# Values of all 40 rows of a segment computed in the softmax wait, in two column groups, in a recurrent-memory transformer block

## The chip, the cores and the metric

One core of one Trainium2 chip. The metric is the device time of one execution of the whole program, in microseconds (us), as the median of several executions. PE is TensorE, DVE is VectorE, ACT is ScalarE, POOL is GpSimd, SP is SyncE, which only issues DMAs here.

## The reference, cut to what matters

A forward and backward pass of a block: layernorm, attention with a recurrent memory, layernorm, gated FFN. The part that this case touches is the forward attention. It walks 64 segments of 32 rows; each segment also sees 8 memory rows, and these are the attention output of the segment before. Segment s + 1 therefore can't start before segment s has ended.

```python
# S = 2048 rows, D = 448, H = 16 heads of 256 (4096 columns), M = 8, seg = 32, L = 40
for s in range(n_seg):                      # 64 dependent steps
    h = concat([mem, x[s*32:(s+1)*32]])     # 40 rows
    q, k, v = h @ Wq, h @ Wk, h @ Wv        # each 40 x 4096
    p = softmax(mask(q k^T * scale))        # per head, 40 x 40
    o = (p v) @ Wo                          # 40 x 448
    mem = o[:8]                             # goes to the next segment
    outs.append(o[8:])
# then h = x + outs, layernorm, FFN, and the gradients of everything
```

Of the kernel before, what the change touches and what calls it, by code (L numbers as in the profile page):

```python
# [15 lines left out]
P = 128  # L16
# [130 lines left out]
def run_all(k: _K):  # L147
    nc, tc, ctx = k.nc, k.tc, k.ctx
    S, D, M, H, Dh, HD, F = k.S, k.D, k.M, k.H, k.Dh, k.HD, k.F
    SEG, L, NSEG, NT, KC, DP, MC, DC, FC = k.SEG, k.L, k.NSEG, k.NT, k.KC, k.DP, k.MC, k.DC, k.FC  # L150
    assert MC == 32 and DC == 2 and H == 16 and M == 8 and NSEG % 16 == 0 and D == 448 and F == 1792
    aps = k.aps
    k.Wq2 = aps["A_Wq"].rearrange("d h e -> d (h e)")
    k.Wk2 = aps["A_Wk"].rearrange("d h e -> d (h e)")
    k.Wv2 = aps["A_Wv"].rearrange("d h e -> d (h e)")
    k.Wo2 = aps["A_Wo"].rearrange("h e d -> (h e) d")

    const = ctx.enter_context(tc.tile_pool(name="const", bufs=1))
    dram = ctx.enter_context(tc.tile_pool(name="dram", bufs=1, space=bass.MemoryType.DRAM))
    k._small = ctx.enter_context(tc.tile_pool(name="small", bufs=4))  # L160
    k.f32p = ctx.enter_context(tc.tile_pool(name="f32", bufs=1))
    arena = ctx.enter_context(tc.tile_pool(name="arena", bufs=1))
    psum = ctx.enter_context(tc.tile_pool(name="psum", bufs=1, space=bass.MemoryType.PSUM))
    k.W = _Arena(arena, "arW", 124)
    k.A = _Arena(arena, "arA", 65)
    k.B = _Arena(arena, "arB", 9.25)
    k.ps1 = lambda: psum.tile([P, 512], FP32, tag="ps", name="psf", bufs=5)
    k.fx1 = lambda: psum.tile([P, 512], FP32, tag="fx", name="fx", bufs=2)
    k.po1 = lambda: psum.tile([P, 512], FP32, tag="po", name="po", bufs=1)
    k.ph1 = lambda: psum.tile([P, 1024], BF16, tag="po", name="ph", bufs=1)  # L170

    def f32(tag, n, name):
        return k.f32p.tile([P, n], FP32, tag=tag, name=name)
    k.f32 = f32

    ident = const.tile([P, P], BF16)
    make_identity(nc, ident[:])
    identf = const.tile([P, P], FP32)
    make_identity(nc, identf[:])
    k.ident = ident  # L180
    k.identf = identf
    sel = const.tile([P, 32], FP32)
    nc.vector.tensor_tensor(out=sel[:], in0=identf[:, 0:32], in1=identf[:, 32:64], op=ALU.add)
    nc.vector.tensor_tensor(out=sel[:], in0=sel[:], in1=identf[:, 64:96], op=ALU.add)
    nc.vector.tensor_tensor(out=sel[:], in0=sel[:], in1=identf[:, 96:128], op=ALU.add)
    k.sel = sel
    maskb = const.tile([P, L], FP32)
    nc.gpsimd.memset(maskb[:], 0.0)
    mask1 = const.tile([L, L], FP32)
    nc.gpsimd.memset(mask1[:], 0.0)  # L190
    nc.gpsimd.affine_select(out=mask1[:], in_=mask1[:], compare_op=ALU.is_ge, fill=-1e9,
                            base=0, pattern=[[-1, L]], channel_multiplier=1)
    nc.gpsimd.memset(mask1[:, SEG:L], 0.0)
    nc.gpsimd.memset(mask1[SEG:L, :], 0.0)
    nc.sync.dma_start(out=maskb[0:L, :], in_=mask1[:])
    nc.sync.dma_start(out=maskb[64:64 + L, :], in_=mask1[:])
    k.maskb = maskb
    eps_t = const.tile([P, 1], FP32)
    nc.gpsimd.memset(eps_t[:], 1e-5)
    k.eps_t = eps_t  # L200
    k.rstd1 = const.tile([P, NT], FP32, name="rstd1")
    k.rstd2 = const.tile([P, NT], FP32, name="rstd2")
    k.mv2 = const.tile([P, NT, nc.vector.BN_AGGR_DIM], FP32, name="mv2")

    def dt(name, shape, dtype=BF16):
        return dram.tile(shape, dtype, name=name)
    W2 = MC * 64
    NB = NT + NSEG // 16
    k.NB = NB
    dr = dict(XN=dt("XN", [NB * P, DP]), Hh=dt("Hh", [S, D]), HN=dt("HN", [S, D]), DH=dt("DH", [S, D], FP32),  # L210
              DHb=dt("DHb", [NB * P, DP]), Zt=dt("Zt", [S, F]), DGP=dt("DGP", [S, F]), DU=dt("DU", [S, F]),
              Vx=dt("Vx", [S, HD]), QT=dt("QT", [NSEG, P, W2]), KT=dt("KT", [NSEG, P, W2]),
              VG=dt("VG", [NSEG, P, W2]), P_all=dt("P_all", [NSEG, P, 8 * L]), DXN=dt("DXN", [S, D], FP32),
              X_o=dt("X_o", [NB, P, MC * P]), HC=dt("HC", [NB * P, DP]))
    for nm in ("q", "k", "v"):
        dr["X_" + nm] = dt("X_" + nm, [NT, P, MC * P])
        dr["M_" + nm] = dt("M_" + nm, [NT, P, MC * 32])
    k.dr = dr

    forward_chain(k)  # L220
    ffn_phase(k)
    backward_chain(k)
    tail_phase(k)
# [39 lines left out]
def forward_chain(k: _K):  # L263
# [17 lines left out]
    stg_b = [A(24 + 4 * i, 2048) for i in range(2)]  # L281
    xblk_b = [A(32 + 8 * i, 32, P) for i in range(2)]
    mblk = A(48, 32, P)
    hT_roll = A(56, KC, NWIN, L)
    hx_b = [A(59.75 + i, KC, P) for i in range(2)]
    v_sb = A(61.75, 1024)
    mh = A(63.75, KC, P)
    memT_pad = B(0, KC, 32)
    PT_bd = B(0.25, 8, 2, L)
    o8_b = [B(1.5 + 0.5 * i, 32, M) for i in range(2)]  # L290
    x2_b = [B(2.5 + 0.875 * i, D) for i in range(2)]
# [4 lines left out]
    nc.vector.memset(qT_b[1][:, :, L:64], 0.0)  # L296
    nc.vector.memset(kT_b[0][:, :, L:64], 0.0)
    nc.vector.memset(kT_b[1][:, :, L:64], 0.0)
    nc.gpsimd.memset(memT_pad, 0.0)
    nc.gpsimd.memset(PT_bd, 0.0)  # L300
    for i in range(2):
        nc.gpsimd.memset(V_b[i], 0.0)
    om = k.f32("f1", DP, "om")
    nc.gpsimd.memset(om[:], 0.0)
    pO = k.po1()
    nc.vector.memset(pO[:], 0.0)

    m0 = h_b[0]
    nc.sync.dma_start(out=v_sb[0:M, 0:D], in_=MEM0)
    nc.vector.memset(v_sb[0:M, D:DP], 0.0)  # L310

    def stats(t):
        q = nc.sync if t % 2 == 0 else nc.scalar
# [16 lines left out]
    pm = k.ps1()  # L330
    pmh = pm[:].bitcast(BF16)
    for kc in range(KC):
        nc.tensor.transpose(pmh[:, kc * M:(kc + 1) * M], v_sb[0:M, kc * P:(kc + 1) * P], ident[0:M, 0:M])
    pm3 = pmh[:, 0:KC * M].rearrange("p (c m) -> p c m", m=M)
    nc.vector.tensor_copy(out=hT_roll[:, :, 0, SEG:L], in_=pm3)
    nc.scalar.copy(out=memT_pad[:, :, 0:M], in_=pm3)
    for t in range(2, NT):
        stats(t)

# [11 lines left out]
    def stg():  # L351
        rot[0] += 1
        return stg_b[rot[0] % 2]

    def v_proj(t, n0, n1):
        if t >= NT:
            return
        for nn in range(n0, n1, 4):
            sg = stg()
            for n in range(nn, nn + 4):  # L360
                pv = k.fx1()
                for kc in range(KC):
                    nc.tensor.matmul(pv[:, 0:512], lhsT=hx_b[t % 2][:, kc, :], rhs=Wv_sb[:, kc, n * 512:(n + 1) * 512],  # L363
                                     start=(kc == 0), stop=(kc == KC - 1))
                k.evac(sg[:, (n - nn) * 512:(n - nn + 1) * 512], pv[:, 0:512])
            nc.gpsimd.dma_start(out=dr["Vx"][t * P:(t + 1) * P, nn * 512:(nn + 4) * 512], in_=sg)

    def load_v(s):
        if s >= NSEG:
            return  # L370
        for g in range(2):
            nc.sync.dma_start(out=V_b[s % 2][64 * g:64 * g + SEG, :],
                              in_=dr["Vx"][s * SEG:(s + 1) * SEG, g * 2048:(g + 1) * 2048])

    def wpass(W_sb, s, dst):
        sl = s % NWIN
# [16 lines left out]
            nc.gpsimd.dma_start(out=dr["X_o"][t][:, hf * 2048:(hf + 1) * 2048], in_=ot)  # L393

    prep_tile(0)
    v_proj(0, 0, 8)
    prep_tile(1)
    v_proj(1, 0, 8)
    load_v(0)
    for s in range(NSEG):  # L400
        t, r = divmod(s, 4)
        jm = s % 16
# [5 lines left out]
        with k.prio.crit():  # L408
# [3 lines left out]
            for h in range(8):  # L412
                for g in range(2):
                    for dc in range(DC):
                        j = 2 * (2 * h + dc) + g
                        nc.tensor.matmul(pS[64 * g:64 * g + 64, h * L:(h + 1) * L], lhsT=qT[:, j, :], rhs=kT[:, j, 0:L],
                                         start=(dc == 0), stop=(dc == DC - 1), skip_group_check=True)
            pV = [k.ps1() for _ in range(2)]
            for b in range(2):
                for kc in range(KC):  # L420
                    for j in range(4):
                        n = 2 * j + b
                        nc.tensor.matmul(pV[b][32 * j:32 * j + 32, 0:512], lhsT=memT_pad[:, kc, :],  # L423
                                         rhs=Wv_sb[:, kc, n * 512:(n + 1) * 512],
                                         start=(kc == 0), stop=(kc == KC - 1), skip_group_check=True)
            S_sb = k.f32("f2", 8 * L, "S_sb")[:].rearrange("p (h n) -> p h n", n=L)
# [4 lines left out]
            nc.vector.tensor_reduce(out=mx[:], in_=S_sb, axis=AX.X, op=ALU.max)  # L431
            nc.vector.tensor_tensor(out=S_sb, in0=S_sb, in1=mx[:].unsqueeze(2).to_broadcast([P, 8, L]), op=ALU.subtract)
            nc.scalar.activation(out=S_sb, in_=S_sb, func=ACT.Exp)
            k.evac(v_sb[:, 0:512], pV[0][:, 0:512], "s")
            k.evac(v_sb[:, 512:1024], pV[1][:, 0:512], "s")
            for j in range(4):
                g = j // 2
                eng = nc.sync if j % 2 == 0 else nc.scalar
                eng.dma_start(out=Vs[64 * g + SEG:64 * g + L, (j % 2) * 1024:(j % 2 + 1) * 1024],
                              in_=v_sb[32 * j:32 * j + M, :])  # L440
            ssum = smal.tile([P, 8], FP32, name="ssum")
            nc.vector.tensor_reduce(out=ssum[:], in_=S_sb, axis=AX.X, op=ALU.add)
            rs = smal.tile([P, 8], FP32, name="rs")
# [26 lines left out]
            if s + 1 < NSEG:  # L470
# [5 lines left out]
                                     start=True, stop=True)  # L476
                pm3 = pm[:, 0:KC * M].rearrange("p (c m) -> p c m", m=M)
                nc.vector.tensor_copy(out=hT_roll[:, :, (s + 1) % NWIN, SEG:L], in_=pm3)
                nc.scalar.copy(out=memT_pad[:, :, 0:M], in_=pm3)

        load_v(s + 1)
        nc.gpsimd.dma_start(out=dr["QT"][s], in_=qT.rearrange("p c n -> p (c n)"))
        nc.sync.dma_start(out=dr["KT"][s], in_=kT.rearrange("p c n -> p (c n)"))
        nc.gpsimd.dma_start(out=dr["P_all"][s], in_=P_sb.rearrange("p h n -> p (h n)"))
# [2 lines left out]
        nc.gpsimd.tensor_copy(out=mblk[:, :, jm * M:(jm + 1) * M], in_=o8)  # L487
        if r == 0:
            prep_tile(t + 2)
        if r % 2 == 1:  # L490
            v_proj(t + 2, 4 * (r // 2), 4 * (r // 2) + 4)
        if r == 3:
            px = k.fx1()
            for j in range(MC):
# [577 lines left out]
```

## The kernel before: the parts that the change and the argument touch

Scheduling is automatic: each engine gets a fixed order of instructions, and `k.prio.crit()` gives what stands in it the first claim. Everything else, such as `v_proj` and the output projection of a finished row tile (`px`, not shown), is put into the gaps as filler. `k.ps1()` takes the next of 5 PSUM banks in turn. `k.evac(..., "s")` copies PSUM to SBUF on ACT, "v" on DVE.

The values of the 32 sequence rows don't depend on memory, so this kernel makes them 128 rows at a time, ahead of need, writes them to DRAM and loads each segment's share:

```python
    def v_proj(t, n0, n1):                  # one row tile of 128 rows, 512 columns at a time
        ...
                for kc in range(KC):
                    nc.tensor.matmul(pv[:, 0:512], lhsT=hx_b[t % 2][:, kc, :], rhs=Wv_sb[:, kc, n * 512:(n + 1) * 512], ...)
                k.evac(sg[:, (n - nn) * 512:(n - nn + 1) * 512], pv[:, 0:512])
            nc.gpsimd.dma_start(out=dr["Vx"][t * P:(t + 1) * P, nn * 512:(nn + 4) * 512], in_=sg)

    def load_v(s):
        for g in range(2):
            nc.sync.dma_start(out=V_b[s % 2][64 * g:64 * g + SEG, :], in_=dr["Vx"][s * SEG:(s + 1) * SEG, g * 2048:(g + 1) * 2048])
```

Only the 8 memory rows' values are made inside the segment. They are made in four column groups of the array, and so land on partitions 0, 32, 64 and 96; four small DMAs move them to partitions 32 and 96 of the value tile:

```python
            wpass(Wq_sb, s, qT); wpass(Wk_sb, s, kT)      # q^T and k^T: 256 small matmuls in all
            ...                                           # scores: 32 matmuls into pS
            pV = [k.ps1() for _ in range(2)]
            for b in range(2):
                for kc in range(KC):
                    for j in range(4):
                        n = 2 * j + b
                        nc.tensor.matmul(pV[b][32 * j:32 * j + 32, 0:512], lhsT=memT_pad[:, kc, :],
                                         rhs=Wv_sb[:, kc, n * 512:(n + 1) * 512], ...)
            ...                                           # scale+mask, max, subtract on DVE
            nc.scalar.activation(out=S_sb, in_=S_sb, func=ACT.Exp)
            k.evac(v_sb[:, 0:512], pV[0][:, 0:512], "s")
            k.evac(v_sb[:, 512:1024], pV[1][:, 0:512], "s")
            for j in range(4):
                g = j // 2
                eng = nc.sync if j % 2 == 0 else nc.scalar
                eng.dma_start(out=Vs[64 * g + SEG:64 * g + L, (j % 2) * 1024:(j % 2 + 1) * 1024],
                              in_=v_sb[32 * j:32 * j + M, :])
            ...                                           # sum, reciprocal, multiply: P_sb
            pPT = k.ps1()                                 # P^T by 16 matmuls with the identity
            for g in range(2):
                k.evac(PT_bd[64 * g:64 * g + L, :, g, :], pPT[64 * g:64 * g + L, ...], "vs"[g])
            ...                                           # heads: 16 matmuls, lhsT = Vs, rhs = PT_bd
            ...                                           # o8 <- memory rows of the heads; pO = o8 @ Wo (32 matmuls)
            ...                                           # om <- pO (DVE, then ACT); sum and transpose; new memory into hT_roll, memT_pad
```

## Time and profile before

| | before |
|---|---|
| time, median of 3 | 3683.66 us (3679.29 to 3687.23) |
| span of the profiled run | 3670.7 us |
| first FFN matmul | 1388 us |
| mean granted clock, 100 to 1388 us | 0.91 |

The top of the page: the span, the busy time of each engine, and the PE clock in 40 slices of the span, in tenths of full speed.

```profile
span 3670.7 us, 122624 instructions
PE 3122.9 (85%) x55484; PEld 2044.1 (56%) x55550; DVE 1349.2 (37%) x2969; ACT 955.4 (26%) x2197; POOL 547.1 (15%) x1177
...
PEclk9999999999999868998799999999999888999999
```

PE looks 85% busy, and its clock is near full almost everywhere, but that alone says nothing about the forward part: there a segment can't overlap the next one, and what counts is which wait ends last in each. The timeline of one segment shows it. Columns: start, duration, engine, line, operation, output and inputs, count, and in brackets the idle time before and what ended it. "SPq" and "PEld" are issuing and weight loading.

```profile
610.75 1.91 PE L423 MATMUL psf<-arW,arB 128*32 128x512 bf16 x31
610.87 0.49 DVE L427 SCALAR_TENSOR_TENSOR S_sb<-psf,maskb 128x320 f32<-128x320 f32 x1 [0.54 <-PE psf L416]
611.84 0.58 ACT L77 CAST arA<-psf 128x512 bf16<-128x512 f32 x1 [2.27 <-PE psf L423]
612.82 0.57 ACT L77 CAST arA<-psf 128x512 bf16<-128x512 f32 x1
613.41 1.51 SPq L439 DMA_DIRECT2D arA<-arA  x2
613.70 0.49 DVE L445 TENSOR_TENSOR arB<-S_sb,rs 128x320 bf16<-128x320 f32 x1
614.25 0.38 PE L449 MATMUL psf<-ident,arB 128*40 128x40 bf16 x16 [1.59 <-DVE arB L445]
615.18 0.42 ACT L77 CAST arB<-psf 40x320 bf16<-40x320 f32 x1 [1.80 <-DVE arB L75]
616.80 0.73 PE L457 MATMUL psf<-arB,arA 128*128 128x80 bf16 x16 [2.18 <-issue]
617.60 3.16 PE L466 MATMUL po<-arW,arB 128*8 128x448 bf16 x32
```

Read it backwards from the heads (L457) at 616.80. P^T was in SBUF at 615.18 + 0.42 = 615.60. The other input is the value tile: its memory rows left PSUM at 613.39, and their DMA was issued at 613.41. So until 1.2 us after P^T is ready PE still idles for a transfer of 64 KB in all. (For this segment the view gives the wait as "issue", that is, it shows no releaser; the list below names the DMA in 29 others.) Then the 32 output-projection matmuls (L466) take 3.16 us; in a segment with filler the same 32 take 1.69 us. The granted clock over those 3.16 us is 0.50 (617.60 to 620.76 in the same trace), so this half rate is the clock, not the work.

The list of waits, PE, from 100 to 1330 us (total us, times, longest):

```profile
PE psf L457 <- DMA arA<-arA: 59.4, 29, 2.7
```

Three groups of instructions over the whole run (count | busy us, mean ns of one | idle before):

```profile
L363 PE MATMUL fx<-arW,arA 128*128 128x512 bf16 x456 | 122.7, 391 | 58.8 <-DMA arA<-XN 39.4
L423 PE MATMUL psf<-arW,arB 128*32 128x512 bf16 x2048 | 150.9, 386 | 1.2 <-issue 1.2
L466 PE MATMUL po<-arW,arB 128*8 128x448 bf16 x2048 | 148.3, 446 | 2.7 <-DVE arB L75 0.3
```

The heads wait 59 us for the DMA where PE stands idle; where filler stands in the order, the wait is hidden but not shorter. L363 is the batched value projection (512 matmuls; some records are missing). L466: 148.3 us for 64 times the same work, of which 64 x 1.69 = 108 us would be full rate.

The end of the chain and the start of the program, timeline lines:

```profile
58.77 10.01 PE L363 MATMUL fx<-arW,arA 128*128 128x512 bf16 x32 [12.37 <-DVE arA L75]
1325.41 7.47 SPq L241 DMA_TRANSPOSE arW<-in_B_w_down_dram  x1
1332.97 2.75 SPq L439 DMA_DIRECT2D arA<-arA  x2
1338.78 1.23 PE L457 MATMUL psf<-arB,arA 128*128 128x80 bf16 x16 [14.91 <-DMA arA<-arA]
```

In the last segment the small value DMA stands behind an FFN weight transpose in SP's queue, and PE waits 14.91 us.

To weigh the parts, every segment was cut at the same DVE instructions. Means over segments 1 to 62, in us, worked out from the timeline (starts of the instructions; for the memory and the probabilities, their ends):

| step | before |
|---|---|
| memory written to scores started (q, k projections, scores) | 8.30 |
| scores to probabilities | 3.35 |
| to the P^T eviction | 0.51 |
| to the first head-output eviction | 2.78 |
| to the copy of the memory rows | 2.72 |
| to the new memory | 2.00 |
| period | 19.67 |

"Half-rate segment" means one in which the fifth step is above 2.8 us; before has 30 of 62. The clock records of the traces bear the name out: in those 30 the granted clock over the output projection is 0.50 to 0.67, in the other 32 it is 1.00.

### The profile page before, as it was taken

The page shows a single profiled execution, that of the slowest core. Times are in us where ns is not written, and L with a number is a line of the kernel's source. Part 1 is how long each engine was busy: PE and PEld are TensorE (multiplying, and loading weights), DVE is VectorE, ACT ScalarE, POOL GpSimd, SP SyncE. Part 2 cuts the span into 40 slices and gives each one's busy share as a digit, 9 for nine tenths or more (in the row PEclk, how much of TensorE's full clock was granted, in tenths as well). Part 3 has the DMA queues.
Part 4 walks back from the last instruction along what each step waited for, and adds up shares of the span by engine and source line. Part 5 has one row for each costly group of instructions (what it writes and reads, how often), then busy time and mean ns, then how long its engine had stood idle before and what let it go on. Part 6 is the DMA issues. An engine that isn't in the chain of part 4 may idle for free.

```text
span 3670.7 us, 122624 instructions
## 1 busy us (share of the span) xinstructions
PE 3122.9 (85%) x55484; PEld 2044.1 (56%) x55550; DVE 1349.2 (37%) x2969; ACT 955.4 (26%) x2197; POOL 547.1 (15%) x1177
## 2 busy tenths in 40 slices
PE   3898888898889847886599999999998776988999
PEld 1666666666666635664466666666666333333444
DVE  3444434344434315675244444444443231111110
ACT  1222222222222212332234344334333001111100
POOL 3111111111111111112021211212111120000000
PEclk9999999999999868998799999999999888999999
DMA  7544544544464387779887867887878888778461
GB/s 250 174 143 156 165 158 149 168 145 153 143 180 151 130 190 168 193 190 222 174 177 168 180 160 166 171 167 161 182 167 224 296 177 166 160 171 156 134 214 55
DMA packets 1028750, 629.13 MB, mean 171 GB/s; under 512 B 910916, under 2 KB 941428, under 8 KB 1026628
## 3 DMA queue, kind: packets, MB, share of 16 engines
q1 hardware_dynamic: 934980, 359.15, 45.7%
q0 software_dynamic: 65888, 238.56, 18.7%
q10 hardware_dynamic: 27360, 23.58, 2.2%
q8 instruction: 435, 7.13, 0.8%
q14 instruction: 87, 0.71, 0.1%
HBM read 124.49 MB, written 270.64 MB: 108 GB/s over the span
## 4 chain that ended last, share of the span: by engine, by line
PE 66%; DMA 12%; DVE 7%; issue 6%; SPq 4%; ACT 4%; POOL 1%; ACTq 0%; DVEq 0%; POOLq 0%
PE psf L382 12%; PE psf L944 8%; PE po L787 6%; PE psf L744 6%; PE po L466 4%; PE psf L722 3%; DMA arA<-arA 3%; PE psf L423 2%; PE fx L846 2%; PE psf L569 2%; PE fx L495 2%; PE fx L949 2%; PE fx L363 2%; PE psf L809 2%; DVE arA L75 2%
## 5 line engine op out<-in xcount | busy, mean ns | idle before, releaser
L75 DVE CAST arA<-psf 128x384 bf16<-128x384 f32 (+6 forms) x1029 | 491.9, 495 | 1002.4 <-PE psf L944 351.2
L77 ACT CAST arA<-psf 128x384 bf16<-128x384 f32 (+6 forms) x1011 | 412.0, 429 | 1475.5 <-PE psf L382 337.1
L382 PEld LDWEIGHTS <-arW 128*128 128x128 bf16 x16384 | 435.4, 98 | 28.9 <-issue 16.8
L382 PE MATMUL psf<-arA,arW 128*128 128x40 bf16 x16384 | 437.5, 182 | 14.6 <-issue 8.0
L787 PE MATMUL po<-arW,arA 128*32 128x448 bf16 x6144 | 346.7, 355 | 21.1 <-DMA arW<-in_A_Wv_dram 21.1
L944 PE MATMUL psf<-arW,arA 128*128 128x512 bf16 x990 | 260.3, 393 | 23.9 <-ACT arA L77 15.4
L944 PEld LDWEIGHTS <-arA 128*128 128x128 bf16 x1440 | 138.9, 101 | 223.1 <-issue 82.9
L744 PE MATMUL psf<-arA,arW 128*128 128x40 bf16 x8192 | 217.9, 180 | 46.0 <-POOL arA L679 40.1
L744 PEld LDWEIGHTS <-arW 128*128 128x128 bf16 x8192 | 214.0, 96 | 65.4 <-issue 64.9
L787 PEld LDWEIGHTS <-arA 128*32 128x32 bf16 x6144 | 152.8, 97 | 131.7 <-issue 22.8
L569 PE MATMUL psf<-arA,arW 128*128 128x256 bf16 x1344 | 163.4, 283 | 72.9 <-DMA arA<-arA 46.4
L569 PEld LDWEIGHTS <-arW 128*128 128x128 bf16 x1344 | 135.9, 101 | 102.6 <-issue 79.0
L363 PE MATMUL fx<-arW,arA 128*128 128x512 bf16 x456 | 122.7, 391 | 58.8 <-DMA arA<-XN 39.4
L75 DVE CAST arB<-psf 40x320 bf16<-40x320 f32 x320 | 107.4, 336 | 165.1 <-PE psf L457 145.8
L965 PE MATMUL psf<-arW 128*128 128x448 bf16 x450 | 101.9, 379 | 59.0 <-DVE arA L75 48.5
L423 PE MATMUL psf<-arW,arB 128*32 128x512 bf16 x2048 | 150.9, 386 | 1.2 <-issue 1.2
L466 PE MATMUL po<-arW,arB 128*8 128x448 bf16 x2048 | 148.3, 446 | 2.7 <-DVE arB L75 0.3
L77 ACT CAST arB<-psf 128x96 bf16<-128x96 f32 (+1 forms) x320 | 98.2, 307 | 200.1 <-PE psf L457 100.2
L457 PE MATMUL psf<-arB,arA 128*128 128x80 bf16 x1024 | 55.6, 216 | 89.8 <-DMA arA<-arA 74.4
L965 PEld LDWEIGHTS <-arW 128*128 128x128 bf16 x606 | 61.8, 102 | 122.2 <-issue 72.4
L754 ACT COPY arA<-psf 128x1024 bf16<-128x1024 bf16 x128 | 123.3, 1015 | 4.8 <-PE psf L753 3.4
L722 PEld LDWEIGHTS <-arW 128*128 128x128 bf16 x2048 | 86.9, 100 | 64.7 <-issue 61.3
(406 smaller groups left out, 4008.9 us busy)
## 6 DMA issues: line engine op xcount, KB each, us to landing
QT<-arA POOLq DMA_DIRECT2D x64, 512.0 KB, 3.9
KT<-arA SPq DMA_DIRECT2D x64, 512.0 KB
VG<-arA SPq DMA_DIRECT2D x64, 512.0 KB
X_o<-arA POOLq DMA_DIRECT2D x40, 512.0 KB, 4.6
Vx<-arA POOLq DMA_DIRECT2D x32, 512.0 KB, 3.2
arA<-Vx SPq DMA_DIRECT2D x128, 128.0 KB
X_v<-arA POOLq DMA_DIRECT2D x32, 512.0 KB, 6.2
X_k<-arA POOLq DMA_DIRECT2D x32, 512.0 KB, 4.0
```

Source lines behind the costliest of these rows:

```text
L75: nc.vector.tensor_copy(out=out, in_=in_)
L77: nc.scalar.copy(out=out, in_=in_)
L363: nc.tensor.matmul(pv[:, 0:512], lhsT=hx_b[t % 2][:, kc, :], rhs=Wv_sb[:, kc, n * 512:(n + 1) * 512], start=(kc == 0), stop=(kc == KC - 1))
L382: nc.tensor.matmul(pss[b][:, jj * L:(jj + 1) * L], lhsT=W_sb[:, kc, c * P:(c + 1) * P], rhs=hT_roll[:, kc, sl, :], start=(kc == 0), stop=( ...
L423: nc.tensor.matmul(pV[b][32 * j:32 * j + 32, 0:512], lhsT=memT_pad[:, kc, :], rhs=Wv_sb[:, kc, n * 512:(n + 1) * 512], start=(kc == 0), st ...
L466: nc.tensor.matmul(pO[32 * (j % 4):32 * (j % 4) + M, 0:D], lhsT=o8[:, j, :], rhs=Wo_sb[:, cj(j), :], start=(j < 4), stop=(j >= MC - 4), sk ...
L569: nc.tensor.matmul(ps[:, f2 * 256:(f2 + 1) * 256], lhsT=Wt[:, kc, c * P:(c + 1) * P], rhs=xT[:, kc, :], start=(kc == 0), stop=(kc == KC - 1))
L722: nc.tensor.matmul(ps[b][:, i * 2 * L:(i + 1) * 2 * L], lhsT=lhs[:, cl, :], rhs=rhs_bd[:, cl // 2, :, :].rearrange("p g n -> p (g n)"), st ...
L744: nc.tensor.matmul(pss[b][:, jj * L:(jj + 1) * L], lhsT=WoT_sb[:, kc, c * P:(c + 1) * P], rhs=do_roll[:, kc, sl, :], start=(kc == 0), stop ...
L787: nc.tensor.matmul(pH[32 * (j % 4):32 * (j % 4) + 32, 0:D], lhsT=blk[nm][:, j, r * SEG:(r + 1) * SEG], rhs=WT[:, cj(j), :], start=(nm == " ...
L944: nc.tensor.matmul(pa[2 * kc + g][:, 0:w], lhsT=lhs_of(b)[:, kc * P:(kc + 1) * P], rhs=rhs_of(b, g), start=(b == 0), stop=(b == nblk - 1), ...
L965: nc.tensor.matmul(pa[i][:, 0:D], lhsT=lhs_of(b, i), rhs=rhs_of(b), start=(b == 0), stop=(b == nblk - 1))
```

## The change

Intent: make the values of all 40 rows inside the segment, in the time in which PE would otherwise wait for the softmax. With 64 stationary columns (40 real ones, 24 of the next window, which P^T's zeros cancel) the output of the two column groups lands on partitions 0 to 63 and 64 to 127, which is where the heads want it. So no DMA has to move it, and the batched projection, its evictions and the DRAM trip go.

```diff
-    hT_roll = A(56, KC, NWIN, L)
+    hT_flat = A(56, KC, NWIN * L + 24)
+    hT_roll = hT_flat[:, :, 0:NWIN * L].rearrange("p k (w l) -> p k w l", l=L)
 ...
-    def v_proj(t, n0, n1): ...
-    def load_v(s): ...
 ...
-            pV = [k.ps1() for _ in range(2)]
-            for b in range(2):
+            pV = [k.ps1() for _ in range(4)]
+            for b in range(4):
                 for kc in range(KC):
-                    for j in range(4):
-                        n = 2 * j + b
-                        nc.tensor.matmul(pV[b][32 * j:32 * j + 32, 0:512], lhsT=memT_pad[:, kc, :],
+                    for g in range(2):
+                        n = 4 * g + b
+                        nc.tensor.matmul(pV[b][64 * g:64 * g + 64, 0:512], lhsT=hT_flat[:, kc, sl * L:sl * L + 64],
                                          rhs=Wv_sb[:, kc, n * 512:(n + 1) * 512],
 ...
-            k.evac(v_sb[:, 0:512], pV[0][:, 0:512], "s")
-            k.evac(v_sb[:, 512:1024], pV[1][:, 0:512], "s")
-            for j in range(4):
-                ... eng.dma_start(out=Vs[64 * g + SEG:64 * g + L, ...], in_=v_sb[32 * j:32 * j + M, :])
+            for b in range(4):
+                k.evac(Vs[:, b * 512:(b + 1) * 512], pV[b][:, 0:512], "s")
 ...
-                nc.scalar.copy(out=memT_pad[:, :, 0:M], in_=pm3)
-        load_v(s + 1)
 ...
-        if r % 2 == 1:
-            v_proj(t + 2, 4 * (r // 2), 4 * (r // 2) + 4)
```

More of the change, by code (lines that the diff above doesn't have):

```diff
@@ L211, in run_all @@
               DHb=dt("DHb", [NB * P, DP]), Zt=dt("Zt", [S, F]), DGP=dt("DGP", [S, F]), DU=dt("DU", [S, F]),
-              Vx=dt("Vx", [S, HD]), QT=dt("QT", [NSEG, P, W2]), KT=dt("KT", [NSEG, P, W2]),
+              QT=dt("QT", [NSEG, P, W2]), KT=dt("KT", [NSEG, P, W2]),
               VG=dt("VG", [NSEG, P, W2]), P_all=dt("P_all", [NSEG, P, 8 * L]), DXN=dt("DXN", [S, D], FP32),
@@ L283, in forward_chain @@
     mblk = A(48, 32, P)
-    hT_roll = A(56, KC, NWIN, L)
-    hx_b = [A(59.75 + i, KC, P) for i in range(2)]
-    v_sb = A(61.75, 1024)
+    hT_flat = A(56, KC, NWIN * L + 24)
+    hT_roll = hT_flat[:, :, 0:NWIN * L].rearrange("p k (w l) -> p k w l", l=L)
+    hx_b = [A(60.25 + i, KC, P) for i in range(2)]
+    m0 = A(62.25, DP)
     mh = A(63.75, KC, P)
-    memT_pad = B(0, KC, 32)
     PT_bd = B(0.25, 8, 2, L)
@@ L298, in forward_chain @@
     nc.vector.memset(kT_b[1][:, :, L:64], 0.0)
-    nc.gpsimd.memset(memT_pad, 0.0)
+    nc.gpsimd.memset(hT_flat[:, :, NWIN * L:], 0.0)
     nc.gpsimd.memset(PT_bd, 0.0)
-    for i in range(2):
-        nc.gpsimd.memset(V_b[i], 0.0)
     om = k.f32("f1", DP, "om")
@@ L306, in forward_chain @@
     nc.vector.memset(pO[:], 0.0)
-    m0 = h_b[0]
-    nc.sync.dma_start(out=v_sb[0:M, 0:D], in_=MEM0)
-    nc.vector.memset(v_sb[0:M, D:DP], 0.0)
+    nc.sync.dma_start(out=m0[0:M, 0:D], in_=MEM0)
+    nc.vector.memset(m0[0:M, D:DP], 0.0)
     def stats(t):
@@ L332, in forward_chain @@
     for kc in range(KC):
-        nc.tensor.transpose(pmh[:, kc * M:(kc + 1) * M], v_sb[0:M, kc * P:(kc + 1) * P], ident[0:M, 0:M])
+        nc.tensor.transpose(pmh[:, kc * M:(kc + 1) * M], m0[0:M, kc * P:(kc + 1) * P], ident[0:M, 0:M])
     pm3 = pmh[:, 0:KC * M].rearrange("p (c m) -> p c m", m=M)
     nc.vector.tensor_copy(out=hT_roll[:, :, 0, SEG:L], in_=pm3)
-    nc.scalar.copy(out=memT_pad[:, :, 0:M], in_=pm3)
     for t in range(2, NT):
@@ L353, in stg @@
         return stg_b[rot[0] % 2]
-    def v_proj(t, n0, n1):
-        if t >= NT:
-            return
-        for nn in range(n0, n1, 4):
-            sg = stg()
-            for n in range(nn, nn + 4):
-                pv = k.fx1()
-                for kc in range(KC):
-                    nc.tensor.matmul(pv[:, 0:512], lhsT=hx_b[t % 2][:, kc, :], rhs=Wv_sb[:, kc, n * 512:(n + 1) * 512],
-                                     start=(kc == 0), stop=(kc == KC - 1))
-                k.evac(sg[:, (n - nn) * 512:(n - nn + 1) * 512], pv[:, 0:512])
-            nc.gpsimd.dma_start(out=dr["Vx"][t * P:(t + 1) * P, nn * 512:(nn + 4) * 512], in_=sg)
-    def load_v(s):
-        if s >= NSEG:
-            return
-        for g in range(2):
-            nc.sync.dma_start(out=V_b[s % 2][64 * g:64 * g + SEG, :],
-                              in_=dr["Vx"][s * SEG:(s + 1) * SEG, g * 2048:(g + 1) * 2048])
     def wpass(W_sb, s, dst):
@@ L395, in forward_chain @@
     prep_tile(0)
-    v_proj(0, 0, 8)
     prep_tile(1)
-    v_proj(1, 0, 8)
-    load_v(0)
     for s in range(NSEG):
@@ L433, in forward_chain @@
             nc.scalar.activation(out=S_sb, in_=S_sb, func=ACT.Exp)
-            k.evac(v_sb[:, 0:512], pV[0][:, 0:512], "s")
-            k.evac(v_sb[:, 512:1024], pV[1][:, 0:512], "s")
-            for j in range(4):
-                g = j // 2
-                eng = nc.sync if j % 2 == 0 else nc.scalar
-                eng.dma_start(out=Vs[64 * g + SEG:64 * g + L, (j % 2) * 1024:(j % 2 + 1) * 1024],
-                              in_=v_sb[32 * j:32 * j + M, :])
+            for b in range(4):
+                k.evac(Vs[:, b * 512:(b + 1) * 512], pV[b][:, 0:512], "s")
             ssum = smal.tile([P, 8], FP32, name="ssum")
@@ L478, in forward_chain @@
                 nc.vector.tensor_copy(out=hT_roll[:, :, (s + 1) % NWIN, SEG:L], in_=pm3)
-                nc.scalar.copy(out=memT_pad[:, :, 0:M], in_=pm3)
-        load_v(s + 1)
         nc.gpsimd.dma_start(out=dr["QT"][s], in_=qT.rearrange("p c n -> p (c n)"))
```

## The prediction

> **What bounds it now.** By the stretch table the forward chain (first FFN matmul at 1388 us) is 38% of the 3671 us span: 64 dependent segments. Cutting vector-engine start times of the timeline at the same marks in every segment, the mean period over segments 1 to 62 is 19.67 us:
> - memory written to scores: 8.30
> - scores to probabilities: 3.35
> - to P-transpose eviction: 0.51
> - to first head-output eviction: 2.78
> - to memory-row copy: 2.72 (2.05 in half the segments, 3.5 in the others)
> - to new memory: 2.00
>
> Two parts are not work. First, memory values go PE → ACT → a partition-moving DMA: in one segment's timeline P^T is evicted at 615.60, the DMA was issued at 613.41, and the head matmuls start only at 616.80. The list of waits shows them held by it for 59 us between 100 and 1330 us, and filler hides more. Second, after such idling the 32 output-projection matmuls take 3.16 us instead of 1.69: half rate, as the Trainium skill, "TensorE: Matmul & The Clock Gate", Part 1, describes for an idle array; the next projections take 7.4 instead of 6.55.
>
> **What changes.** PE work is about equal: value matmuls in four column groups (32 in 1.9 us, starts 51 ns apart) become 32 in two groups. The skill's "TensorEngine Tiling (Array Packing)" gives two independent tiles for 64 columns; the tail's 64-column pairs agree (8 in 0.99 us at clock 0.86). Estimate: 108 ns each at full clock, 3.5 us per segment. The scores-to-P^T wait is about 3.9 us, so they fit. Removed: 512 full-width value matmuls (about 110 us of PE, partly filler), their evictions, 33.6 MB of DRAM traffic, 256 small value DMAs. Added: two 0.58 us ACT evictions per segment; the built order puts Exp after the first and the P^T eviction after the fourth, which I expect to delay P^T by at most 0.2 us.
>
> **On the path, per segment.** P^T to heads 2.78 → 1.5 (no DMA; filler there is now only six 0.19 us matmuls). Warm array (longest idle about 1 us): memory-row copy 2.72 → 2.1, projections 8.30 → 7.9. Period 17.4 us; 63 × 2.27 ≈ 143 us.
>
> **Ends.** Prologue: two tiles of value projection and their evictions, stuck behind layernorm statistics (idle to 58.8 us), leave the path; first memory 92.4 → about 70 (−22). Last segment: the value DMA sits in the SyncE queue behind FFN weight transposes, PE idle 14.9 us; that goes, and the FFN input transposes now precede one weight transpose, but other transposes take part back: −15. FFN, backward, tail: ±5.
>
> **Predicted: 3508 us (−4.8%), range 3460 to 3570.** Faster by over 2%: 0.95; within 2%: 0.04; slower: 0.01.
>
> **Right or wrong in the profile.** Forward period 17.2 to 17.7 us, spread under 1 us; no DMA releasing the head matmuls; output projection about 1.7 us in nearly all segments; value matmuls 105 to 115 ns apart, ending before P; forward granted clock above 0.93; first FFN matmul near 1210.
>
> **What would make it wrong.** 64-column pairs not overlapping (7 us, period +3.5: near the old time); ACT's order delaying Exp or P^T; the removed filler having kept the array warm; unexplained "issue" stalls of about 1 us in the projections growing; prologue evictions still waiting for statistics; the queue after the chain giving the gain back before the FFN.

## The result, and the profile after

| | before | after |
|---|---|---|
| time, median | 3681.47 us (3670.55 to 3687.23, 4 runs) | 3517.76 us (3504.09 to 3532.75, 4 runs) |
| ratio, 95% interval | | 0.956, 0.9514 to 0.9606 |
| span of the profiled run | 3670.7 us | 3502.3 us |
| mean granted clock of the forward part | 0.91 | 0.97 |

A ratio is the mean time of one kernel's fast runs over that of the other's of the same rounds, so it is not quite the ratio of the medians quoted.

The top of the page of after, span and PE clock. In tenths the forward part, the first third, looks the same as before (9 means 90% or more); only the means, 0.91 and 0.97, tell the two apart:

```profile
span 3502.3 us, 120836 instructions
...
PEclk8999999999999799987999999999999889999999
```

One segment's timeline of after, the lines that answer those of before:

```profile
610.09 3.62 PE L397 MATMUL psf<-arW,arA 128*64 128x512 bf16 x30
610.28 0.49 DVE L401 SCALAR_TENSOR_TENSOR S_sb<-psf,maskb 128x320 f32<-128x320 f32 x1 [0.40 <-PE psf L389]
611.15 0.59 ACT L77 CAST arA<-psf 128x512 bf16<-128x512 f32 x1 [2.01 <-PE psf L397]
612.29 1.18 ACT L77 CAST arA<-psf 128x512 bf16<-128x512 f32 x2
613.17 0.49 DVE L414 TENSOR_TENSOR arB<-S_sb,rs 128x320 bf16<-128x320 f32 x1
613.72 0.38 PE L418 MATMUL psf<-ident,arB 128*40 128x40 bf16 x16
613.74 0.59 ACT L77 CAST arA<-psf 128x512 bf16<-128x512 f32 x1 [0.28 <-PE psf L397]
614.71 0.42 ACT L77 CAST arB<-psf 40x320 bf16<-40x320 f32 x1 [0.38 <-DVE arB L75]
615.18 0.73 PE L426 MATMUL psf<-arB,arA 128*128 128x80 bf16 x16 [1.08 <-ACT arB L77]
615.97 1.69 PE L435 MATMUL po<-arW,arB 128*8 128x448 bf16 x32
```

The value matmuls fill the wait to the brim: they end at 613.71, the probabilities at 613.66. 30 matmuls in 3.62 us, less the 0.38 us that the last one runs, are 29 steps of 112 ns: two at a time. The fourth eviction ends at 614.33, ahead of P^T at 615.13, and the heads start 0.05 us after P^T. Measured from the start of the scores' scaling, P^T is ready after 4.85 us here and after 4.73 before, so the two extra evictions cost 0.12 us. The output projection takes 1.69 us, at a granted clock of 1.00.

Waits of PE from 60 to 1150 us:

```profile
PE psf L426 <- ACT arB L77: 35.0, 32, 1.4
```

Groups:

```profile
L397 PE MATMUL psf<-arW,arA 128*64 128x512 bf16 x2048 | 258.5, 381 | 0.0
L435 PE MATMUL po<-arW,arB 128*8 128x448 bf16 x2048 | 109.4, 356 | 4.1 <-DVE arB L75 0.4
```

No DMA is among the releasers of the heads any more; they wait for the ACT half of P^T. The output projection has gone from 148.3 to 109.4 us with nothing changed in it.

The start, and the end of the chain, timeline lines of after:

```profile
52.27 0.63 DVE L82 BATCH_NORM_STATS2 stats<-arA 128x6 f32<-128x448 bf16 x1 [18.07 <-DMA arA<-in_A_x_dram]
59.93 1.23 PE L358 MATMUL psf<-arA,arW 128*128 128x40 bf16 x32 [10.74 <-DVE arA L75]
1172.77 6.23 PE L460 MATMUL fx<-arW,arA 128*128 128x448 bf16 x32
1223.67 12.24 PE L534 MATMUL psf<-arA,arW 128*128 128x256 bf16 x96 [44.67 <-DMA arA<-arA]
```

| step of a segment, mean us | before | after |
|---|---|---|
| to scores | 8.30 | 7.89 |
| to probabilities | 3.35 | 3.40 |
| to P^T eviction | 0.51 | 0.47 |
| to heads | 2.78 | 1.52 |
| to copy of memory rows | 2.72 | 2.05 |
| to new memory | 2.00 | 2.00 |
| period | 19.67 | 17.34 |
| half-rate segments of 62 | 30 | 0 |

| stage, us | before | after | difference |
|---|---|---|---|
| start to first memory | 92.4 | 81.8 | −10.6 |
| 62 segments | 1219.3 | 1075.3 | −144.0 |
| last segment, to the first FFN matmul | 76.5 | 66.6 | −9.9 |
| FFN | 365.6 | 365.8 | +0.2 |
| backward chain | 1094.4 | 1101.6 | +7.2 |
| tail | 822.6 | 811.2 | −11.4 |

The last two stages don't contain the change. Over all profiles the backward chain took 1090 to 1104 us and the tail 802 to 823, so differences of this size there are scatter. The gain is in the 62 segments. Of the 2.33 us gained in each, 1.26 are the shorter step to the heads, 0.67 and 0.41 the steps with the output projection and with the projections that follow it.

### The profile page after: what moved, and what is told of

Its sections match the earlier page's. It is cut to its first block, busy times and chain, and to the rows that moved or that the text cites. A ratio compares the mean times of both kernels' runs of the same rounds, so it can differ in the third digit from the quotient of the medians.

```text
span 3502.3 us, 120836 instructions
## 1 busy us (share of the span) xinstructions
PE 3045.6 (87%) x55028; PEld 2059.0 (59%) x55038; DVE 1320.4 (38%) x2905; ACT 982.4 (28%) x2197; POOL 533.5 (15%) x1143
## 4 chain that ended last, share of the span: by engine, by line
PE 69%; DMA 9%; DVE 8%; issue 7%; SPq 4%; ACT 3%; POOL 1%; ACTq 0%; DVEq 0%; POOLq 0%
PE psf L358 12%; PE psf L909 8%; PE po L752 7%; PE psf L709 6%; PE psf L397 6%; PE psf L687 3%; PE po L435 3%; PE fx L460 3%; PE fx L811 2%; PE psf L534 2%; PE fx L914 2%; PE psf L774 2%; DVE arA L75 2%; PE psf L718 2%; PE fx L909 2%
## 5 line engine op out<-in xcount | busy, mean ns | idle before, releaser
L77 ACT CAST arA<-psf 128x320 bf16<-128x320 f32 (+4 forms) x1139 | 486.5, 447 | 1533.6 <-PE psf L358 423.0
L909 PE MATMUL psf<-arW,arA 128*128 128x512 bf16 x990 | 261.3, 394 | 10.6 <-DVE arA L75 6.6
L397 PE MATMUL psf<-arW,arA 128*64 128x512 bf16 x2048 | 258.5, 381 | 0.0
L397 PEld LDWEIGHTS <-arA 128*64 128x64 bf16 x2048 | 147.6, 111 | 65.2 <-issue 0.2
L460 PE MATMUL fx<-arW,arA 128*128 128x448 bf16 x512 | 124.5, 353 | 0.0
L687 PE MATMUL psf<-arB,arW 128*128 128x80 bf16 x2048 | 97.2, 201 | 19.3 <-DVE arB L736 7.5
```

Of the source, the lines that this page charges most:

```text
L77: nc.scalar.copy(out=out, in_=in_)
L397: nc.tensor.matmul(pV[b][64 * g:64 * g + 64, 0:512], lhsT=hT_flat[:, kc, sl * L:sl * L + 64], rhs=Wv_sb[:, kc, n * 512:(n + 1) * 512], sta ...
L460: nc.tensor.matmul(px[:, 0:D], lhsT=xblk[:, j, :], rhs=Wo_sb[:, cj(j), :], start=(j == 0), stop=(j == MC - 1))
L687: nc.tensor.matmul(ps[b][:, i * 2 * L:(i + 1) * 2 * L], lhsT=lhs[:, cl, :], rhs=rhs_bd[:, cl // 2, :, :].rearrange("p g n -> p (g n)"), st ...
L909: nc.tensor.matmul(pa[2 * kc + g][:, 0:w], lhsT=lhs_of(b)[:, kc * P:(kc + 1) * P], rhs=rhs_of(b, g), start=(b == 0), stop=(b == nblk - 1), ...
```

## The experiments

Theory A: the gain is the handover PE → ACT → DMA → PE taken off the chain, directly and through the half-rate PE that follows the idling. Rival B: it is the 512 batched matmuls that no longer run. Rival C: it is the DRAM traffic, and the queues that it filled. "Chain" is the time from the first memory to that of segment 62, from one profile.

### Handover off the chain, everything else kept

```diff
-                eng.dma_start(out=Vs[64 * g + SEG:64 * g + L, ...
+                eng.dma_start(out=V_b[(s + 1) % 2][64 * g + SEG:64 * g + L, ...
```

> Before, but the partition-moving DMA of the memory values writes the other value buffer, so they arrive one segment late (outputs wrong on purpose) and no head matmul waits for this segment's DMA. All PE work, evictions and DRAM traffic stay. Theory A (most of the gain is the handover PE to ACT to DMA to PE taken off the chain, directly and through the half-rate PE that follows the idling): P^T eviction to first head-output eviction falls from 2.78 to about 1.6 us, segments with a half-rate output projection from 30 to at most 15 of 62, the 14.9 us stall of the last segment goes, period about 18.2 us, total 85 to 115 us shorter. Rival B (the gain is the 512 batched value matmuls that no longer run): at most 30 us shorter. Rival C (the gain is the DRAM traffic and the queues it filled): at most 30 us shorter.

Measured: 3580.08 us, ratio 0.9733 (0.9699 to 0.9767), 102 us shorter than before on the same chip. P^T to heads 1.59 us, 12 half-rate segments, period 18.48, chain 1145.8 us (before: 1219.3). The outputs passed the comparison although each segment multiplies by the memory values of the one before: presumably their share of the result is too small for the tolerance. So the comparison is no witness for this edit. The output projection's group:

```profile
L466 PE MATMUL po<-arW,arB 128*8 128x448 bf16 x2048 | 124.9, 392 | 3.5
```

All 512 batched matmuls and all DRAM traffic are still there, and 62% of the gain has come (102 of 164 us). By the chain, which leaves the ends out, it is 73.5 of 144 us, about half. B and C allowed 30 us. In the last segment the heads waited 1.03 us, for P^T, where before they waited 14.91.

### No batched matmuls, handover and DRAM trip kept

```diff
-            sg = stg()
-            for n in range(nn, nn + 4):
-                ... 4 matmuls, eviction
-            nc.gpsimd.dma_start(out=dr["Vx"][...], in_=sg)
+            nc.gpsimd.dma_start(out=dr["Vx"][...], in_=Wv_sb[:, t % 3, nn * 512:(nn + 4) * 512])
```

> Before without the 512 batched value matmuls and their evictions; the DRAM trip stays, fed with a slice of a weight (outputs wrong on purpose). Theory A: those matmuls were filler in waits that stay, so the P^T-to-heads step stays at 2.5 to 2.8 us and, with less filler, at least as many segments (30 or more of 62) run half-rate: total 0 to 40 us shorter, of which about 10 in the prologue. Rival B: about 110 us shorter or more, period near 18. Rival C: no more than the prologue's 10 us.

Measured: 3712.19 us, ratio 1.0082 (1.0054 to 1.011), that is 30 us longer than before; outputs wrong, as meant. Period 20.60, P^T to heads 2.91, 49 half-rate segments instead of 30. Waits of PE, from 100 to 1370 us:

```profile
PE psf L451 <- DMA arA<-arA: 104.7, 45, 4.2
```

The output projection's group:

```profile
L460 PE MATMUL po<-arW,arB 128*8 128x448 bf16 x2048 | 175.3, 510 | 1.9 <-DVE arB L75 0.2
```

As long as the handover stands, rival B has fallen with the sign against it: taking away 110 us of PE work made the program longer. Theory A had the mechanism (filler in waits that stay, more half-rate segments) but not the sign of the total: I expected 0 to 40 us shorter and had not added up what 19 more half-rate segments cost.

### No batched matmuls and no DRAM trip

```diff
     def v_proj(t, n0, n1): / def load_v(s):
+        pass          # and V_b is filled once with a constant
```

> As the run without batched matmuls, and the DRAM trip of the values taken away too; the values of the rows are a constant (outputs wrong on purpose). Memory values still go through ACT and the partition-moving DMA. Theory A: within 15 us of the run that keeps the DRAM trip. Rival C: at least 40 us shorter than it, with the memory-value DMA landing sooner and the P^T-to-heads step shorter by 0.5 us or more.

Measured: 3717.09 us, ratio 1.0089 (1.0059 to 1.012), within 5 us of the run that keeps the trip. Period 20.38 against 20.60, P^T to heads 2.83 against 2.91: small, and not in the total. (The first FFN matmul came 18 us sooner, 1418.8 against 1437.0 us, but later stages, which the edit doesn't touch, were 23 us longer in this profile.) C asked for 40 us and for 0.5 us in that step. Rival C has fallen, at least as long as the handover is there.

### Dead matmuls to keep the array busy

```diff
+            pdead = k.ps1()
+            for rep in range(8):
+                for j in range(4):
+                    nc.tensor.matmul(pdead[32 * j:32 * j + 32, 0:512], lhsT=memT_pad[:, rep % KC, :], rhs=Wv_sb[...], ...)
```

> Before with 32 dead four-column-group matmuls (about 1.7 us of PE) added behind the memory-value matmuls in the softmax wait; nothing else changes, outputs right. Theory A, its second half (half-rate PE after idling costs about 0.7 us in the output projection and 0.4 in the next projections, on average): no segment with an output projection above 2.8 us, period shorter by 0.8 to 1.2 us, P^T-to-heads step still about 2.7, total 40 to 70 us shorter although PE does 110 us more. If the half rate does not come from the idling, or added PE work is on the chain: no change or up to 110 us longer.

Measured: 3677.00 us, ratio 0.999 (0.9951 to 1.0029): no change. Half-rate segments fell from 30 to 7 and the output projection from 148.3 to 119.0 us. In the last segment of each row tile, which before had no filler in the softmax wait or ahead of the heads, the mean period fell from 20.55 to 18.40 us (some of the batched matmuls now fall there too, so not all of this need be the dead ones). But the new order pushed the batched matmuls from the softmax wait into the one before the heads, the median period fell only to 18.54 (before 19.91), and single segments piled up: one took 48.8 us. There the eviction of the heads waited for POOL to release its buffer, and POOL stood in front of a store that waited for a DMA transpose:

```profile
767.22 0.54 POOL L393 DMA_DIRECT2D X_o<-arA  x1 [7.22 <-DMA arA<-arA]
768.20 0.24 ACT L77 CAST arB<-psf 128x96 bf16<-128x96 f32 x1 [21.71 <-POOL arA L493]
```

So the half rate does follow the idling: that rests on the count of half-rate segments. The expected total was missed, and "no change" was the outcome that the expectation gave to the other theory. The four longest periods lie 54 us above the median together, so the pile-ups can have given much of the gain back.

### The same dead matmuls, without the batched ones

The edits of the second and the fourth run together.

> The run without batched value matmuls (DRAM trip kept, handover by DMA kept, outputs wrong on purpose), with the 32 dead four-column-group matmuls of the warm run in the softmax wait. Its PE work per segment is thus that of the changed kernel; what it still has against it is the DMA handover. Theory A: hardly any half-rate segment (49 of 62 without the dead matmuls), period 18.4 to 18.9 us, P^T-to-heads step still about 2.7; total 100 to 125 us shorter than the run without them, and 60 to 100 us longer than the changed kernel. If half rate is not caused by idling: no shorter than the run without them.

Measured: 3677.62 us, ratio 1.0007 (0.9963 to 1.0051). Against the run without dead matmuls (1.0082) that is about 0.7%, where I expected 3%. Half-rate segments 28 instead of 49, chain 1227.8 instead of 1277.4 us. Two timeline lines show why it is not more:

```profile
622.10 0.73 PE L457 MATMUL psf<-arB,arA 128*128 128x80 bf16 x16 [2.30 <-DMA arA<-arA]
622.90 3.16 PE L466 MATMUL po<-arW,arB 128*8 128x448 bf16 x32
```

The softmax wait is now filled, as in the changed kernel, but the handover alone still leaves PE idle for 2.30 us, and here the half rate follows (granted clock 0.50). In the second segment of each row tile, segment 1 left out, none is half-rate, and the period is 18.28 us: 1.1 us above that of the same segments in the changed kernel (17.19), and the step to heads (2.65 against 1.52) holds that difference.

### The changed kernel with the handover put back

```diff
             for b in range(4):
                 k.evac(Vs[:, b * 512:(b + 1) * 512], pV[b][:, 0:512], "s")
+            for j in range(4):                 # rows 48 to 55 of each group meet zeros in P^T
+                eng.dma_start(out=Vs[64 * g + 48:64 * g + 48 + M, ...], in_=Vs[64 * g + SEG:64 * g + L, ...])
```

> The changed kernel with the handover put back: after the four value evictions the same four small partition-moving DMAs (8 rows x 1024 columns, two on each queue) write rows of the value tile that the head matmuls multiply by zeros, so the heads wait for them and the outputs stay right. Theory A: the last value eviction ends about 4.0 us after the scores and the DMA needs about 3.4 us from there, so the P^T-to-heads step grows from 1.52 to about 4 us, half-rate segments come back in about half of the segments, period 20 to 22 us, total 150 to 280 us longer than the changed kernel: the gain is gone or worse. Rivals B and C (no batched matmuls, no DRAM trip, both still true here): at most 20 us longer than the changed kernel.

Measured: 3726.75 us, ratio 1.015 (1.0105 to 1.0194): 209 us longer than the changed kernel's 3517.76 (217 by the two ratios, since the rounds differ), and 50 us longer than before on the same chip. Period 20.61. The fifth step is above 2.8 us in 49 segments, but only in 39 of them is the granted clock over the output projection reduced (0.68 or less); in the other 10 it is 1.00, and the step is long because the second half of the heads lies in it. The step to heads is 2.83, not 4: the DMAs of the first 1024 columns are issued after the second of the four evictions and overlap the rest. The second half of the heads comes 2.0 us later and lands in the next step, which has grown to 3.74. One segment, timeline:

```profile
631.25 1.33 SPq L413 DMA_DIRECT2D arA<-arA  x2
632.78 1.31 ACTq L413 DMA_DIRECT2D arA<-arA  x2
634.14 0.42 ACT L77 CAST arB<-psf 40x320 bf16<-40x320 f32 x1 [1.38 <-DMA arA<-arA]
634.61 0.45 PE L431 MATMUL psf<-arB,arA 128*128 128x80 bf16 x8 [2.15 <-ACT arB L77]
636.61 0.71 PE L431 MATMUL psf<-arB,arA 128*128 128x80 bf16 x8
```

What the first half of the heads waits for here is ACT's half of P^T, and ACT came to it only after it had issued two of the DMAs (632.78 to 634.09); DVE's half was done at 632.98. In before the same issuing ended (614.70) ahead of ACT's half (615.18). So the 209 us are the handover with ACT's time to issue it, at a later place than in before; no run separates the parts. The output projection's group; its busy time, 180.3 us, is the longest:

```profile
L440 PE MATMUL po<-arW,arB 128*8 128x448 bf16 x2048 | 180.3, 443 | 16.8 <-DVE arB L75 16.8
```

With this run a table of two by two is complete. Chains in us:

| | handover on the chain | handover off |
|---|---|---|
| batched projection runs | 1219.3 (before) | 1145.8 (handover late) |
| no batched projection | 1277.4 (before without it), 1277.7 (after with handover) | 1075.3 (after) |

The two kernels without batched projection and with the handover, one made from before and one from after, agree to 0.3 us, which is closer than such chains repeat (the changed kernel's: 1075.3 and 1083.1). That is luck, for they differ in two ways that offset each other: the second fills the softmax wait, which made the first 50 us shorter in the run with dead matmuls (1227.8), and its handover starts later. The handover costs 73.5 us where filler covers part of it and 202 us in the changed kernel with it put back. Leaving out the batched projection loses 58 us while the handover is on the chain. The 70.5 us between the two cells on the right are not for leaving it out alone: after also has the longer value matmuls in the softmax wait. A before without batched projection and with the handover late was not run. Neither part has a worth of its own.

### The changed kernel with the batched projection run for nothing

```diff
+        if r % 2 == 1:
+            v_proj(t + 2, 4 * (r // 2), 4 * (r // 2) + 4)     # as before; nobody reads Vx
```

> The changed kernel with the batched value projection of 14 of the 16 row tiles run again for nothing: 448 full-width matmuls (97 us of PE at full rate), their evictions and the store to DRAM, nobody reads it; outputs right. Theory A: the 16 matmuls per half tile have hardly any idle PE left to fall into, so about 1.2 us in each of 28 segments, total 20 to 60 us longer than the changed kernel, P^T-to-heads step below 1.8. Rival B (their removal is the gain): 100 us longer or more.

Measured: 3582.51 us, ratio 0.9744 (0.9704 to 0.9783), 65 us longer than the changed kernel (68 by the ratios). It is just above A's range, and far below B's 100. The chain is 1139.0 us, 64 longer. Two segments hold most of it: number 34 took 47.1 us and number 50 took 31.8, together 44 us above twice the changed kernel's mean period. The median period is 17.66 against 17.13, and P^T to heads is 1.52 us in the median. Segment 34, timeline:

```profile
707.23 0.39 DVE L75 CAST arB<-psf 128x96 bf16<-128x96 f32 x2 [16.90 <-POOL arA L467]
707.54 3.15 PE L448 MATMUL po<-arW,arB 128*8 128x448 bf16 x32 [17.01 <-DVE arB L75]
```

It is the pile-up of the dead-matmul run again. The batched projection shares its two staging buffers with the transposed blocks that are stored every 4 segments, and with further ones every 16. So part of what its removal brings is not PE time but a free staging ring; these two segments show it, no run isolates it.

### P^T in two PSUM banks (tried as an improvement)

What ends last before the heads is now the pair of P^T evictions: DVE 0.48 us, then ACT 0.42. The built program has ACT wait for DVE, since both read one bank. The Trainium skill, "PSUM — Partial Sum Buffer", section "PSUM bank collisions raise a hardware error", says that two engines on one bank and the same 32 partitions must be kept apart; different banks, or other groups of 32 partitions in one bank, need no such guard. The two halves lie on partitions 0 to 39 and 64 to 103, so by that page one bank would do; the wait is the built program's, and two banks are a way around it.

```diff
-            pPT = k.ps1()
+            pPT = [k.ps1() for _ in range(2)]
...
-                    nc.tensor.matmul(pPT[64 * g:64 * g + L, ...
+                    nc.tensor.matmul(pPT[g][64 * g:64 * g + L, ...
```

> The changed kernel with the transposed probabilities of the two head groups in two PSUM banks instead of one, so that the ACT eviction of one half does not wait for the VectorE eviction of the other. What now ends last before the heads is that pair: VectorE 0.48, then ACT 0.42 us. ACT is free about 0.38 us before it starts now. Expected: P^T-to-heads step 1.52 to about 1.15 us, period 17.34 to about 17.0, total about 23 us (0.65%) shorter than the changed kernel. If the PSUM rotation (one buffer more per segment) or the fourth value eviction is the limit: no change.

Measured: 3504.89 us, ratio 0.9533 (0.9497 to 0.9569). P^T to heads 1.19, period 17.10, chain 1060.1 us. ACT now starts 0.23 us after DVE instead of after its end:

```profile
610.33 0.48 DVE L75 CAST arB<-psf 40x320 bf16<-40x320 f32 x1 [0.46 <-PE psf L418]
610.56 0.42 ACT L77 CAST arB<-psf 40x320 bf16<-40x320 f32 x1
```

Three runs beside each other on one chip followed, to read half a per cent.

> The changed kernel as it is, run once more beside the next two, so that a difference of half a per cent can be read on one chip. Expected: 3500 to 3530 us, forward period 17.3 us, first memory at about 82 us.

> The changed kernel with the transposed probabilities in two PSUM banks, beside the changed kernel itself. Expected from its first run (period 17.10 against 17.34, P^T-to-heads 1.19 against 1.52): 10 to 25 us shorter than the changed kernel, about 0.5%.

Measured: the changed kernel again 3524.67 us, ratio 0.9543 (0.9519 to 0.9568), chain 1083.1; two banks 3510.93 us, ratio 0.9508 (0.9487 to 0.9529), chain 1059.1. P^T to heads 1.52 and 1.18 as in the first pair. The chain is 24 us shorter, as worked out; the medians differ by 14 us (0.4%), and the intervals of the two ratios still overlap slightly. In this profile PE's wait for the first FFN matmul was 14 us longer, 63.2 against 48.9 us, and took part of it back.

### Two banks, and the output-projection weights loaded later

```diff
-    nc.gpsimd.dma_start(out=Wo_sb, ...)        # after the loads of Wq, Wk, Wv
     ...
     prep_tile(0)
     prep_tile(1)
+    nc.gpsimd.dma_start(out=Wo_sb, ...)
```

> The two-bank version, and the load of the output-projection weights issued only after the first row tiles are in place (about 47 us instead of 18 us), to test what holds the prologue. The prediction put the first memory at 70 us and it came at 81.8: the first projections wait 10.7 us for VectorE, which waits in order for layernorm statistics of row tiles whose loads crawl beside the weight loads (one issued at 31.7 us landed at 52.3). Expected if so: those loads land about 10 us sooner, first memory at 70 to 75 us, total 8 to 12 us shorter than the two-bank version. If the loads are slow for another reason: first memory stays at 80 to 84 us. If the weights come too late for the first output projection: later than 84 us.

Measured: 3507.55 us, ratio 0.9499 (0.9477 to 0.9521), the lowest ratio but not apart from the two-bank version's. First memory at 79.8 us, a miss: expected 70 to 75. The theory of the loads was half right:

```profile
39.93 0.63 DVE L82 BATCH_NORM_STATS2 stats<-arA 128x6 f32<-128x448 bf16 x1 [5.88 <-DMA arA<-in_A_x_dram]
55.06 0.40 DVE L317 TENSOR_SCALAR arA<-arA,mv,rstd 128x448 bf16<-128x448 bf16 x1 [11.87 <-DMA XN<-arA]
```

The row load issued at 31.6 us was there at 39.9 instead of 52.3, but then DVE, still ahead of the first projection's eviction, waited 11.87 us for the store of a normalised tile to free its buffer. The stores crawl like the loads did. What would free the first eviction is a DVE order in which it doesn't stand behind the statistics; that was not tried.

## Why the prediction was right

**The total.** Predicted 3508 us, range 3460 to 3570; measured 3517.76. The gain was put at 180 us before the open ±5, and the profiled spans differ by 168.4.

**The segments: right, in size and in parts.** Predicted period 17.4, measured 17.34. P^T to heads 1.5 → 1.52; memory-row copy 2.1 → 2.05; projections 7.9 → 7.89; 143 us over the chain → 144.0. The late handover and the two-by-two table show that the handover is a cause, and that leaving out the batched matmuls was worth nothing as long as it stood. That the half rate is one too is shown by the dead matmuls without the batched ones: 28 half-rate segments instead of 49, and a chain 50 us shorter with nothing but dead matmuls added, 32 us of it in the step with the output projection. How much of the gain in the changed kernel comes from the filled softmax wait and how much from the missing handover was not separated.

**Two column groups overlap: right.** The skill's two tiles for 64 columns ("TensorEngine Tiling (Array Packing)", Tiling Modes) and the estimate of 108 ns from the tail agree with 112 ns. (The pairs in the tail start 4 and 213 ns apart at a granted clock of 1.00; the 0.86 quoted with them is the mean of a longer stretch.) They were to end before the probabilities; they end with them (613.71 and 613.66 us). There is no slack left in that wait.

**ACT's order: right.** At most 0.2 us late was expected, 0.12 us measured in one segment without filler. Over all 62 segments P^T is ready 4.87 us after the start of the scaling, before 4.96.

**The array stays warm: right.** No half-rate segment among the 62 (one, segment 1, in the second profile of this kernel), granted clock of the forward part 0.97 (above 0.93 was expected), output projection 109.4 us for 64. Middle 80% of the periods 16.99 to 17.85, under 1 us; all but three lie below 17.9, and the longest, segment 1, is 20.1.

**The prologue: mis-sized.** "First memory 92.4 → about 70 (−22)"; measured 81.8, −10.6. The batched projection left the path, but the first q and k evictions stand in the same DVE order behind the same statistics: PE idles 10.74 us for them. The prediction named it among what would make it wrong ("prologue evictions still waiting for statistics"). The last run shows that the row loads are not the whole reason; the stores of the normalised tiles hold the same buffers.

**The end: a little mis-sized.** −15 predicted, −9.9 measured; first FFN matmul at 1223.7 instead of "near 1210", of which the prologue is the larger part. The 14.91 us stall is gone, but PE's wait between the last forward output projection and the first FFN matmul has grown from 38.1 to 44.7 us, so 6.5 us were given back. That transposes did it, as feared, is likely (one of the FFN weights holds SP's queue for 16.27 us there, from 1193.44) but not shown: before has such transposes there too.

**Missed on the way.** I gave the removed batched matmuls a gain of their own in the second experiment (0 to 40 us shorter; it was 30 us longer), 100 to 125 us to dead matmuls that brought about 28 (0.75% by the two ratios), and no weight to the staging buffers that they share with other stores.

## What to carry to other kernels

In a dependent chain, count what ends last in each step, not what keeps the engines busy: here 110 us of matmuls removed alone made the program slower, and the same removal together with one small DMA made it 4.4% faster. When a result has to change partitions before its next use, look for a matmul shape whose output lands where it is needed, even if it spends more PE time, as long as that time lies in a wait. After idling, work that nobody touched can run at half rate (here 3.16 us instead of 1.69, at a granted clock of 0.50), so check its duration before and after, not only the wait.

## What the Trainium skill lacked or had wrong

- "TensorE: Matmul & The Clock Gate", Part 1 ties the half rate to an idle window of about 3.4 us, and the advice under "Why this matters for your kernels" is to have no gap longer than about 3 us. (The page's "A second HAM failure mode" tells of frequent short idling that does it too, without a figure for how much.) Here a gap of 2.30 us, with PE busy for 2.70 of the 5 us ahead of the heads, was followed by the half rate (3.16 us instead of 1.69 for the same 32 matmuls, granted clock 0.50). Worked out from the PE records of before: the 30 output projections with a reduced clock had PE busy for 1.85 of the 5 us ahead of them on average (largest gap 2.10 us on average, never above 2.67), the 32 at full clock for 4.35 us. These are averages and no threshold: the ranges are 1.12 to 3.16 and 2.52 to 4.94 us.
- "DMA: Bandwidth & Descriptors", section "Anatomy of one DMA — SWDGE (gpsimd) path", gives about 2.0 us of fixed cost for a DMA issued by POOL. For the partition-moving SBUF-to-SBUF handover issued by SP and ACT, which no page that I found costs as a link of a chain, before shows 3.4 us from the first issue to the dependent matmul, issue included (613.41 to 616.80; the median is 3.38 over the 29 segments in which the view names this DMA as what the heads waited for).
- No page gives a number for what filler matmuls are worth in a dependent chain by keeping the array at full rate: with the handover in place the chain was 58 us longer without the batched ones, and 50 us shorter again with dead ones in the softmax wait.
